# Adding the global keys of batch 0 by short matmuls instead of copying their value rows

**The chip, the cores and the metric.** One core of one Trainium2 chip (trn2). The metric is the device time of one execution in microseconds (us), from the core's first to its last instruction plus a constant start and end; lower is better. Most executions of one kernel lie within 0.3% of each other, so each one is measured against runs of the kernel before on the same chip. "Faster" and "slower" below mean only that the 95% interval of the ratio leaves 1 out.

Engines: PE is TensorE (matmuls), PEld its weight loads, DVE VectorE, ACT ScalarE, POOL GpSimd, SP SyncE. `L670` is line 670 of the kernel at hand; the same statement has another line number before and after.

## The reference, cut to what matters

```python
batch, n_heads, seq, head_dim = (8, 8, 576, 64)      # q, k, v
n_global = 8                                         # global_idx: 8 sorted positions
mask = np.abs(pos[:, None] - pos[None, :]) <= 32     # a window of 32 to each side ...
mask = mask | is_global[:, None] | is_global[None, :]  # ... plus 8 global rows and columns
attn = softmax(where(mask, q @ k.T / sqrt(64), -1e9))
x = (attn @ v).transpose(0, 2, 1, 3).reshape(4608, 512)
h = x @ w_in                                         # 512 -> 2048
out = (maximum(h, 0) ** 2) @ w_out                   # 2048 -> 512
```

So every query sees its window and the eight global keys. The kernel lays the keys of a batch out in five tiles of 128 rows. Rows 0 to 7 of each tile are the global keys, the others are window keys. One matmul with 128 contraction rows then adds both kinds.

## The kernel before

Attention runs batch by batch, in four pairs of heads, each in two halves of the queries. Everything from batch 1 on fills PE with expert units (`x @ w_in` and `g @ w_out`, in pieces held in a queue). Batch 0 has little expert work to put beside it, so its own chain is exposed there. That chain begins with the global value rows, which are not known by position until the index has been read (the code is cut, and comments are added):

```python
    def pick_values():                       # one-hot matmuls: the 8 global rows of V
        gp = pst("mm", [P, 512])[0:NG]
        for x in range(NT):
            nc.tensor.matmul(gp.rearrange(...), oh[:, x, :], vb[0][:, x, 0 : 2 * H : 2],
                             start=(x == 0), stop=(x == NT - 1))
        dve.tensor_copy(out=gv16, in_=gp.rearrange("p (h d) -> p h d", d=D))

    def spread_values(b, op, tiles=range(NT)):     # ... into rows 0..7 of the value tiles
        for x in tiles:
            op(out=vb[b][0:NG, x, 0 : 2 * H : 2], in_=gv16)
# ... (cut)
    pick_values()
    spread_values(0, dve.tensor_copy, range(0, 4))
    spread_values(0, act.copy, range(4, NT))
    masked(0, ets[2], WIN)
    masked(0, ets[3], WIN)
    # ... (cut: load issues on POOL, then:)
    next_in_place()                          # POOL casts gathered rows for batch 2
    keep_warm(SCHED["w7"])                   # fillers on PE
    half0_out(0, "mm")                       # outputs and reciprocals, pairs 0 to 3
    half0_out(1, "sc")
    half0_out(2, "acc")
    half0_out(3, "mm")
    # ... (cut: scores of half 1 of pairs 0, 1)
    scatter(0, 0)                            # global query columns into xT, half 0
    # ... (cut: half 1 of the four pairs, expert units between them)
    scatter(0, 1)
    take(len(queue) - SCHED["keep"])         # all queued expert units but `keep`
```

The sums of the softmax come from the same matmuls with a tile of ones in place of V; ACT takes a logarithm and an exponential of minus it to get the reciprocal. `scatter` copies eight columns per half into `xT`, the input of the expert units, so no expert unit of that half can start before it.

The softmax here doesn't subtract the row's maximum and nothing guards it: scores larger than these inputs give would overflow.

## Time and profile before

| | kernel before |
|---|---|
| time, median of the runs first given | 326.37 us |
| PE busy, share of the span | 97% |
| granted clock | 1.00 |
| picks start (L449) | 15.91 us |
| first expert unit starts | 25.79 us |
| first scatter | 23.86 to 25.74 us |
| second scatter | 36.08 to 38.53 us |

The table of waits gives, for each group, who it waited for, then the us in total, how often, and the longest. These are its lines for PE that the change could touch:

```profile
PE mm L543 <- DVE xT L751: 1.8, 2, 1.2
...
PE mm L524 <- DVE xT L751: 0.5, 1, 0.5
...
PE mm L670 <- DVE vb L457: 0.4, 1, 0.4
```

The two waits of L543 are those for the two scatters of batch 0, L524's is for the scatter of batch 1, and L670's is for the copied rows. Together 2.7 us.

### The profile page before, as it was taken

How to read it: one execution, taken by the hardware profiler on the slowest of the kernel's cores; microseconds unless marked ns; L12 is line 12 of the kernel's file. 1: busy time of each engine (PE TensorE's matmuls, PEld its weight loads, DVE VectorE, ACT ScalarE, POOL GpSimd, SP SyncE). 2: the span in 40 equal slices, each digit the busy share in tenths (PEclk: the TensorE clock that was granted, in tenths of full speed). 3: DMA queues.
4: the chain of work that ended last, by engine and by line, in shares of the span. 5: the costliest groups of instructions: out<-in, count | busy, mean ns of one | idle time of the engine just before them, and what ended most of it. 6: DMA issues, size and time to landing. Idle time of an engine off the chain costs nothing.

```text
span 326.0 us, 6920 instructions
## 1 busy us (share of the span) xinstructions
PE 316.8 (97%) x2434; PEld 164.5 (50%) x2434; DVE 227.0 (70%) x674; ACT 214.4 (66%) x418; POOL 110.2 (34%) x148
## 2 busy tenths in 40 slices
PE   6998999999999999999999999999999999999996
PEld 2645775445555455455545544454455544444444
DVE  7786987677878875987598758885888675313421
ACT  6677985569954995499549954995499636404600
POOL 9824663639800870089107700680000000000000
PEclk9999999999999999999999999999999999999999
DMA  8999999999994999399959996999610011011012
GB/s 186 176 204 190 174 186 167 154 147 107 153 131 141 73 138 171 134 83 139 132 162 82 148 126 144 98 134 132 139 60 0 34 58 39 2 73 56 2 54 75
DMA packets 148229, 37.53 MB, mean 115 GB/s; under 512 B 136171, under 2 KB 143715, under 8 KB 148195
## 3 DMA queue, kind: packets, MB, share of 16 engines
q0 software_dynamic: 105168, 17.93, 78.9%
q1 hardware_dynamic: 42880, 19.04, 30.3%
q8 instruction: 19, 0.31, 0.4%
q10 hardware_dynamic: 146, 0.13, 0.1%
q14 instruction: 16, 0.12, 0.1%
HBM read 37.30 MB, written 17.05 MB: 167 GB/s over the span
## 4 chain that ended last, share of the span: by engine, by line
PE 88%; DVE 7%; ACT 2%; issue 1%; DMA 1%
PE mm L587 29%; PE mm L524 26%; PE tr L524 9%; PE tr L587 7%; PE sc L679 3%; PE acc L679 3%; PE sc L627 3%; PE mm L543 2%; PE acc L627 2%; DVE xT L751 2%; PE tr L197 1%; DVE vb L457 1%; PE sc L670 1%; DVE xT L732 1%; ACT rec L702 1%
## 5 line engine op out<-in xcount | busy, mean ns | idle before, releaser
L587 PE MATMUL mm<-w_out,gt 128*128 128x512 f16 x448 | 104.4, 379 | 0.0
L524 PE MATMUL mm<-xT,w_in 128*128 128x512 f16 x384 | 90.8, 379 | 0.5 <-DVE xT L751 0.5
L587 PEld LDWEIGHTS <-gt 128*128 128x128 f16 x560 | 52.4, 98 | 58.6
L524 PEld LDWEIGHTS <-w_in 128*128 128x128 f16 x512 | 47.5, 98 | 53.7 <-issue 0.8
L529 ACT ACTIVATE rl<-mm 128x512 f16<-128x512 f32 x96 | 54.3, 599 | 26.7 <-PE mm L524 26.7
L530 DVE TENSOR_TENSOR gt<-rl 128x512 f16<-128x512 f16 x128 | 51.0, 422 | 17.0 <-ACT rl L529 15.6
L636 ACT ACTIVATE et<-sc 128x880 f16<-128x880 f32 (+1 forms) x32 | 29.0, 907 | 44.1 <-PE sc L627 39.1
L643 DVE TENSOR_TENSOR et<-et,mask 128x880 f16<-128x880 f16 (+1 forms) x64 | 38.9, 615 | 24.1 <-ACT et L636 23.8
L113 POOL DMA_DIRECT2D vb<-in_v_dram x40 | 40.7, 1532 | 9.0 <-DMA w_in<-in_moe_w_in_dram 7.3
L524 PE MATMUL tr<-xT,w_in 128*128 128x512 f16 x128 | 33.0, 380 | 0.0
L564 DVE COPY ot<-mm 128x512 f32<-128x512 f32 (+1 forms) x29 | 19.7, 680 | 18.0 <-PE mm L587 16.3
L636 ACT ACTIVATE et<-acc 128x880 f16<-128x880 f32 (+1 forms) x32 | 29.1, 909 | 1.0 <-PE acc L627 1.0
L703 ACT ACTIVATE rec<-rec 128x288 f32<-128x288 f32 x64 | 28.3, 443 | 2.0
L732 DVE TENSOR_TENSOR xT<-sc,rec 64x288 f16<-64x288 f32 (+1 forms) x55 | 25.0, 455 | 6.5 <-ACT rec L703 6.2
L732 DVE TENSOR_TENSOR xT<-acc,rec 64x288 f16<-64x288 f32 (+1 forms) x55 | 25.0, 455 | 3.9 <-ACT rec L703 1.1
L404 POOL DMA_DIRECT2D scr_k<-in_k_dram x30 | 26.6, 1111 | 2.8 <-issue 2.8
L679 PEld LDWEIGHTS <-vb 128*128 128x128 f16 x288 | 21.3, 98 | 11.5
L930 POOL COPY pin<-gsh 1x1 f32<-1x1 f32 x5 | 0.9, 177 | 76.4 <-DVE gsh L720 76.4
L702 ACT ACTIVATE rec<-sc 64x288 f32<-64x288 f32 (+1 forms) x55 | 22.3, 406 | 6.2 <-PE sc L679 4.2
L404 POOL DMA_DIRECT2D scr_q<-in_q_dram x24 | 25.1, 1585 | 3.0 <-DMA w_out<-in_moe_w_out_dram 3.0
L587 PE MATMUL tr<-w_out,gt 128*128 128x512 f16 x112 | 25.3, 379 | 0.0
L702 ACT ACTIVATE rec<-acc 64x288 f32<-64x288 f32 (+1 forms) x55 | 22.2, 404 | 2.0 <-PE acc L670 1.1
(147 smaller groups left out, 308.5 us busy)
## 6 DMA issues: line engine op xcount, KB each, us to landing
out_dram<-ot SPq DMA_DIRECT2D x35, 256.0 KB
vb<-in_v_dram POOLq DMA_DIRECT2D x32, 120.0 KB, 11.3
scr_q<-in_q_dram POOLq DMA_DIRECT2D x24, 144.0 KB, 5.9
scr_k<-in_k_dram POOLq DMA_DIRECT2D x24, 120.0 KB, 4.2
w_in<-in_moe_w_in_dram POOLq DMA_DIRECT2D x4, 512.0 KB, 11.9
w_out<-in_moe_w_out_dram POOLq DMA_DIRECT2D x4, 512.0 KB, 12.3
natk<-in_k_dram POOLq DMA_DIRECT2D x3, 288.0 KB, 10.9
natq<-in_q_dram POOLq DMA_DIRECT2D x3, 288.0 KB, 15.8
```

The lines of the kernel that those rows point to most:

```text
L113: pool.dma_start(out=vb[b][NG : NG + KN[x], x, 2 * hs.start : 2 * hs.stop : 2], in_=v[b, hs, x * KT : x * KT + KN[x]].rearrange("h s d -> ...
L404: pool.dma_start(out=scr[(nm, b % 2)][x * pitch + off : x * pitch + off + hi - lo].rearrange("s (h d) -> s h d", d=D), in_=src[nm][b, :, l ...
L524: nc.tensor.matmul(ph, w_in[:, t, u * P : (u + 1) * P], xT[:, t, XOFF + c * TC : XOFF + (c + 1) * TC], start=(t == 0), stop=(t == NDM - 1),)
L529: nc.scalar.activation(out=rl, in_=ph, func=AF.Relu)
L530: nc.vector.tensor_tensor(out=gts[c][:, u, :], in0=rl, in1=rl, op=ALU.mult)
L587: nc.tensor.matmul(po, gts[c][:, f, m * P : (m + 1) * P], w_out[:, f, :], start=(f == 0), stop=(f == NFF - 1),)
L636: act.activation(out=et[:, :, 0:W], in_=sc[:, :, 0:W], func=AF.Exp, bias=0.0, scale=scale)
L643: dve.tensor_tensor(out=et[:, :, 0:W], in0=et[:, :, 0:W], in1=mask[:, MB[half] : MB[half] + W].unsqueeze(1).to_broadcast((P, 2, W)), op=AL ...
L679: nc.tensor.matmul(banks[e][:, o : o + w], vtf[:, t, vo : vo + P], et[:, e, so : so + w], start=(n == 0), stop=(n == nw - 1), skip_group_c ...
L702: act.activation(out=rec[r], in_=av[xs][rs, :, 0:GTOK], func=AF.Ln)
L703: act.activation(out=rec, in_=rec, func=AF.Exp, scale=-1.0)
L732: dve.tensor_tensor(out=xT[r, hp, x0 : x0 + HS].rearrange("p (k x) -> p k x", k=2), in0=av[x][r, :, 0:GTOK], in1=rec[r], op=ALU.mult,)
```

## The change

Its intent: take the copies out of the chain. The value tiles keep zeros in rows 0 to 7. The eight rows stay in `gv16`, and matmuls with a contraction of 8 (K=8) add the global keys to each output afterwards. The window part of the outputs need not wait for them, nor need the denominators. With the time gained, fillers are taken out.

```diff
-SCHED = dict(... w7=4, wa=4, wb=3, wc=3, ... w=5, h0=0, ... h2=1, h3=0, keep=1, ...)
+SCHED = dict(... w7=0, wa=4, wb=2, wc=1, ... w=3, h0=1, ... h2=0, h3=0, keep=2, ...)
-    def pick_values():
-        gp = pst("mm", [P, 512])[0:NG]
+    def pick_values(part):                   # two picks of four heads each
+        gp = pst("mm", [P, 512])[0:NG, 0:256].rearrange("p (h d) -> p h d", d=D)
... (cut)
+    def global_keys(i, half, et, banks, wins):
... (cut: own = the column ranges of the three windows whose global keys are in use)
+        for n, (off, lo_, hi_) in enumerate(own):
+            for e in range(2):
+                nc.tensor.matmul(
+                    banks[0][D * e : D * e + D, lo_ - half * BANKC : hi_ - half * BANKC],
+                    gv16[:, 2 * hp + e], et[0:NG, e, off + lo_ : off + hi_],
+                    start=False, stop=(n == len(own) - 1), skip_group_check=True,
+                )
... (cut)
-    pick_values()
-    spread_values(0, dve.tensor_copy, range(0, 4))
-    spread_values(0, act.copy, range(4, NT))
     masked(0, ets[2], WIN)
-    masked(0, ets[3], WIN)
+    pick_values(0)
+    pick_values(1)
+    first = [pst("mm", [P, 512]), pst("tr", [P, 512])]
+    column_outputs(0, 0, ets[0], first, WIN, slice(None))
... (cut: load issues, next_in_place() as before)
-    keep_warm(SCHED["w7"])
-    half0_out(0, "mm")
... (cut)
+    reciprocals(0, first, True)
+    second = output_banks("sc")
+    column_outputs(1, 0, ets[1], second, WIN, slice(None))
+    masked(0, ets[3], WIN)
+    global_keys(0, 0, ets[0], first, WIN)
+    global_keys(1, 0, ets[1], second, WIN)
... (cut: pairs 2 and 3 with their global_keys; half 1 likewise)
```

More of the change, by code (lines that the diff above doesn't have):

```diff
@@ L42 @@
 MB = (0, 456)
-SCHED = dict(w8=2, w9=3, w5=3, w6=0, w7=4, wa=4, wb=3, wc=3, g0=1, w0=2, w1=4, w2=2, w3=2, w4=3, w=5, h0=0, h1=1, h4=1, h5=1, h2=1, h3=0, keep=1, b1=((3, 1, 3), (2, 1, 3), (2, 1, 3), (2, 1, 2)), last=((2, 1, 4), (3, 1, 4), (2, 1, 4), (2, 1, 7)))
+SCHED = dict(w8=2, w9=3, w5=3, w6=0, w7=0, wa=4, wb=2, wc=1, g0=1, w0=2, w1=4, w2=2, w3=2, w4=3, w=3, h0=1, h1=1, h4=1, h5=1, h2=0, h3=0, keep=2, b1=((3, 1, 3), (2, 1, 3), (2, 1, 3), (2, 1, 2)), last=((2, 1, 4), (3, 1, 4), (2, 1, 4), (2, 1, 7)))
 ONES = 2.0**-7 * (1.0 + 15360.0 / 2**23)
@@ L444, in clear_value_rows @@
         )
-    def pick_values():
-        gp = pst("mm", [P, 512])[0:NG]
+    def pick_values(part):
+        gp = pst("mm", [P, 512])[0:NG, 0:256].rearrange("p (h d) -> p h d", d=D)
+        hs = slice(4 * part, 4 * part + 4)
         for x in range(NT):
             nc.tensor.matmul(
-                gp.rearrange("p (h d) -> p h d", d=D), oh[:, x, :], vb[0][:, x, 0 : 2 * H : 2],
+                gp, oh[:, x, :], vb[0][:, x, 8 * part : 8 * part + 8 : 2],
                 start=(x == 0), stop=(x == NT - 1),
             )
-        dve.tensor_copy(out=gv16, in_=gp.rearrange("p (h d) -> p h d", d=D))
+        dve.tensor_copy(out=gv16[:, hs], in_=gp)
     def spread_values(b, op, tiles=range(NT)):
@@ L654, with output_banks, column_outputs @@
     PARTS = (((lo, 0, hi, 0), (hi, 1, lo, 1)), ((slice(0, P), 0, slice(0, P), 1),))
-    def outputs(i, half, et, tag, wins, columns=False):
-        b, hp = divmod(i, NHP)
-        if tag == "mm":
-            banks = [pst("mm", [P, 512]) for _ in range(2)]
-        else:
-            acc = pst(tag, [P, 2, 512])
-            banks = [acc[:, x] for x in range(2)]
-        vt = vb[b]
-        vtf = vt.rearrange("p t x d -> p t (x d)")
+    def output_banks(tag):
+        if tag == "mm":
+            return [pst("mm", [P, 512]) for _ in range(2)]
+        acc = pst(tag, [P, 2, 512])
+        return [acc[:, x] for x in range(2)]
+    def column_outputs(i, half, et, banks, wins, some):
+        b, hp = divmod(i, NHP)
         nw = len(wins[half])
-        for n, (t, so, c0, w) in enumerate(wins[half] if columns else ()):
+        for n, (t, so, c0, w) in list(enumerate(wins[half]))[some]:
             o = c0 - half * BANKC
@@ L671, in outputs @@
                         banks[x][D * e : D * e + D, o : o + w],
-                        one64 if x else vt[:, t, 4 * hp + 2 * e], et[:, e, so : so + w],
-                        start=(n == 0), stop=(n == nw - 1), skip_group_check=True,
-                    )
-        for e in () if columns else range(2):
+                        one64 if x else vb[b][:, t, 4 * hp + 2 * e], et[:, e, so : so + w],
+                        start=(n == 0), stop=(n == nw - 1 and (b > 0 or x > 0)),
+                        skip_group_check=True,
+                    )
+    def global_keys(i, half, et, banks, wins):
+        b, hp = divmod(i, NHP)
+        own = []
+        for t, so, c0, w in wins[half]:
+            cs = [
+                (max(KT * t + 8 * grp, GRP * grp, c0),
+                 min(KT * (t + 1) + 8 * grp, GRP * grp + GTOK, c0 + w))
+                for grp in range(4)
+            ]
+            cs = [c for c in cs if c[0] < c[1]]
+            if cs:
+                own.append((so - c0, cs[0][0], cs[-1][1]))
+        for n, (off, lo_, hi_) in enumerate(own):
[5 more added lines that the diff above has]
+                )
+    def outputs(i, half, et, tag, wins, columns=False):
+        b, hp = divmod(i, NHP)
+        banks = output_banks(tag)
+        if columns:
+            column_outputs(i, half, et, banks, wins, slice(None))
+            if b == 0:
+                global_keys(i, half, et, banks, wins)
+            return banks
+        vt = vb[b]
+        vtf = vt.rearrange("p t x d -> p t (x d)")
+        nw = len(wins[half])
+        for e in range(2):
             for n, (t, so, c0, w) in enumerate(wins[half]):
@@ L694, in global_outputs, with reciprocals @@
             )
+    recs = {}
+    def reciprocals(i, acc, columns):
+        rec = recs[i] = sbt("rec", [P, 2, GTOK], FP32, bufs=4)
+        for r, x, rs, xs in PARTS[columns]:
+            den = acc[xs][rs, 0:BANKC].rearrange("p (k c) -> p k c", c=GRP)
+            act.activation(out=rec[r], in_=den[:, :, 0:GTOK], func=AF.Ln)
+        act.activation(out=rec, in_=rec, func=AF.Exp, scale=-1.0)
     def finish_outputs(i, half, acc, columns=False):
@@ L699, in finish_outputs @@
         av = [a[:, 0:BANKC].rearrange("p (k c) -> p k c", c=GRP) for a in acc]
-        rec = sbt("rec", [P, 2, GTOK], FP32, bufs=4)
-        for r, x, rs, xs in parts:
-            act.activation(out=rec[r], in_=av[xs][rs, :, 0:GTOK], func=AF.Ln)
-        act.activation(out=rec, in_=rec, func=AF.Exp, scale=-1.0)
+        if i not in recs:
+            reciprocals(i, acc, columns)
+        rec = recs.pop(i)
         if b == 0:
@@ L712, in finish_outputs @@
                     )
-                if hp >= NHP - 2:
-                    a, z = (0, NHP - 1) if hp < NHP - 1 else (NHP - 1, NHP)
-                    global_outputs(0, gsum[0], a, z, columns)
+                if hp == NHP - 1:
+                    global_outputs(0, gsum[0], 0, NHP, columns)
         else:
@@ L784, in half0 @@
         ets[i] = exps(0, scores(i, 0, tag, WIN), WIN)
-    def half0_out(i, tag):
-        acc = outputs(i, 0, ets[i], tag, WIN, columns=True)
-        finish_outputs(i, 0, acc, columns=True)
     half0(0)
@@ L822 @@
     next_in_place()
-    keep_warm(SCHED["w7"])
-    half0_out(0, "mm")
-    half0_out(1, "sc")
-    half0_out(2, "acc")
-    half0_out(3, "mm")
+    reciprocals(0, first, True)
[4 more added lines that the diff above has]
+    global_keys(1, 0, ets[1], second, WIN)
+    finish_outputs(0, 0, first, columns=True)
+    finish_outputs(1, 0, second, columns=True)
+    for i, tag in ((2, "acc"), (3, "mm")):
+        finish_outputs(i, 0, outputs(i, 0, ets[i], tag, WIN, columns=True), columns=True)
     def half1(i):
```

## The prediction

> **What bounds the kernel now.** I read the page first, then the chain of waits in order of time for the stretch 14 to 50 us, then the timeline around it, the table of waits, and the busy table by stretch. First lines of the page and two lines of the busy table (us, then each engine's busy time):
>
> ```profile
> PE 316.8 (97%) x2434; PEld 164.5 (50%) x2434; DVE 227.0 (70%) x674; ACT 214.4 (66%) x418; POOL 110.2 (34%) x148
> ...
> 15.00:20.00 5.00, 4.03 (x69) 2.21 (x63) 3.20 (x12) 3.19 (x6) 2.45 (x4) 1.00 1.27 205
> 20.00:26.00 6.00, 4.84 (x72) 2.59 (x67) 5.36 (x26) 5.64 (x13) 1.82 (x2) 1.00 1.28 204
> ```
>
> TensorE (PE) is busy for 97% of the span. From 46 us to the end nothing but PE work counts; the change touches none of that. Only a stretch in which PE is idle, or busy with nothing of use, can give time back, and batch 0 is one: between 15 and 26 us PE is idle 2.1 us, and part of its busy time is filler (L197, matmuls on an idle tile that only keep the clock up). The chain there (start, us, what):
>
> ```profile
> 15.97 1.19 PE mm L449 x5
> 17.16 0.02 issue
> 17.18 0.69 DVE gv L453
> 17.88 0.02 issue
> 17.90 1.33 DVE vb L457 x4
> 19.23 0.04 issue
> 19.27 0.32 PE mm L670 x8
> 19.59 0.02 issue
> 19.62 0.42 ACT rec L702
> ...
> 25.79 1.03 PE mm L543 x8
> ```
>
> The eight global value rows are picked (L449), copied to fp16 (L453), copied into rows 0 to 7 of five value tiles (L457), and only then can the outputs of pair 0 (L670) end and their reciprocals (L702, L703) start. After that ScalarE (ACT) and VectorE (DVE) pass four pairs, DVE scatters the global columns (L751), and at 25.79 the first expert unit (L543) starts. The timeline shows what DVE could have done meanwhile, and who waited for the scatter:
>
> ```profile
> 17.18 0.68 DVE L453 CAST gv<-mm 8x512 f16<-8x512 f32 x1 [1.76 <-PE mm L449]
> ...
> 19.14 1.15 DVE L643 TENSOR_TENSOR et<-et,mask 128x912 f16<-128x912 f16 x2
> ...
> 25.79 1.03 PE L543 MATMUL mm<-xT,w_in 128*128 128x256 f16 x8 [1.16 <-DVE xT L751]
> ```
>
> DVE idles 1.76 us ahead of the copy although one of the two masks (L643, et of pair 2) could be had from 16.4 on: its exponential starts at 15.41 and takes 0.95.
>
> **What the Trainium skill says.** "TensorE: Matmul & The Clock Gate", section "Why this matters for your kernels": a matmul with 32 contraction rows takes as long as one with 128. So I price the K=8 matmuls by their columns. The trace has no K=8 matmul, but it gives the price of columns: in the pair of column outputs from 19.42 on, two matmuls of 160 columns for both heads start 0.07 us after the ones before, 192 columns 0.08, 88 and 8 columns 0.03 to 0.035.
> The same page, Part 1: an idle window of about 3.4 us halves the clock. The trace shows a granted clock of 1.00 through an idle gap of 1.16 us. Nine fillers go, but no gap gets near 3.4 us, so I expect the clock to stay 1.00.
> "PSUM — Partial Sum Buffer", section "PSUM bank collisions raise a hardware error": two engines must not touch one bank at once. The trace agrees: DVE's sum of pair 1 (L709) starts at 20.91, after ACT's logarithm of the same bank (20.41, 0.39). So ACT paces the four pairs, at 0.77 us each (20.41, 21.18, 21.95).
> "SBUF — State Buffer", section "Who interferes with whom": DVE copies that use the shared port pair and GpSimd (POOL) shut each other out. The trace agrees: the eight copies of the second scatter (36.08) take 2.45 us beside three POOL casts, and one of the first takes 0.42 instead of 0.19 beside a POOL issue at 24.23. Without it the first scatter is 8 x 0.21 = 1.7 us.
>
> **The change part by part.**
> (1) Removed: the five row copies, 1.33 us of DVE on the chain and 0.62 of ACT beside it.
> (2) The pick becomes two picks of half the columns: ten matmuls, the same 1.1 to 1.2 us of PE. The copy becomes two of 256 columns. 8x512 takes 0.68; taking 0.15 of that as fixed, a half is 0.42, so 0.8 for both: 0.1 more.
> (3) Moved: the mask of pair 2 goes ahead of the copies, into the 1.76 us idle (0.6 saved). The outputs of pair 0 go directly behind the picks on PE, with denominators in another bank than values, and its reciprocal no longer waits for any global row.
> (4) Added: six K=8 matmuls per pair and half, 120, 128 and 48 columns in half 0, 72, 128 and 96 in half 1: about 0.05 + 0.055 + 0.033 = 0.14 us for both heads; eight times, 1.1 us of PE.
> (5) The two small global divisions (L690, L692) become one: 0.20 + 0.17 less, 0.05 more for its extra columns.
> (6) Fillers on PE: w7 4 to 0, wb 3 to 2, wc 3 to 1, w 5 to 3: nine fewer at 0.21 = 1.9 us. One expert unit moves between the two half-1 outputs (h0) from behind pair 2 (h2), and one more stays queued for batch 1 (keep 2), which hands the same PE work on.
>
> New path, step by step: picks end near 17.1; DVE masks pair 2 at 16.4 to 17.0, copies to about 17.75, masks pair 3 to 18.3. PE passes pair 0's outputs by 17.5 and pair 1's by 18.0, then the global matmuls of both by 18.3. ACT takes the logarithm of pair 0 at 17.7 instead of 19.62. Pair 1's logarithm must wait for its global matmuls, as its banks are one tile: 18.5. Then ACT's pace: 18.5, 19.27, 20.05 for pairs 1, 2 and 3, where the kernel before has 20.41, 21.18 and 21.95: 1.9 us earlier. The last exponential ends at 20.9; sum, division, last product: 21.8; scatter 1.7: 23.5. The first expert unit starts at 23.5 instead of 25.79: 2.3 us earlier.
>
> From there to the scatter of half 1 it is PE that counts. Two fillers fewer (0.4) against four times 0.13 of global matmuls: 0.1 to 0.2 later. So the half-1 outputs end some 2.1 us earlier, near 32.5. One unit that ran before batch 1's scores now runs behind them; as PE is full from there on, that is neutral, if it fills the wait for the second scatter. Before, PE idled 0.64 us for that scatter; here I allow 0.3 for the scores of the first pair of batch 1, which must wait for a bank, and nothing else.
>
> The sum in PE time between 15 and 46 us, as a second count: fillers -1.9, global matmuls +1.1, idle from about 2.8 (0.97 + 1.16 + 0.64) to about 1.7. That is -1.9 us. The two counts agree on **1.9 us, so 324.5 us**.
>
> **The rivals.**
> R1, the loads become the bound. GpSimd's issues wait for the transfer eight places back, which gives landing times: w_in's four parts at 18.20, 20.40, 24.23 and 26.60, the first values of batch 1 at 34.72. The expert units that use w_in would run at 23.5 at the earliest on parts 1 and 2, and near 30 on part 3: landed. The batch-1 values are nearer: from 34.72 to 45.85, where the third w_out part lands, four value parts and three of w_out went through; at 2.1 us per w_out part (as w_in) the values take 1.2 each, so the last lands near 39.4. Its first use would move from 42.6 to about 40.1. It just fits; if it doesn't, 0.5 to 1 us is lost: 325.3.
> R2, the global matmuls cost more than their columns (a weight load of few rows that does not hide, 12 instructions in a burst). At 0.3 us instead of 0.14 eight times this takes 1.3 back, some of it in gaps: 325.4.
> R3, the second scatter keeps its end. It sits beside POOL casts whose start hangs on loads (35.5 to 37.2), not on compute; moved 2 us ahead it may meet a w_out issue as well as the casts, and PE, out of units of half 0, waits: 0.3 to 0.7 lost. For: the 2.45 us above. Against: with keep 2 there is one unit more to fill.
> R4, everything hidden by PE: the page's 97% speaks for it, but the 2.1 us idle and the fillers lie in this very stretch, so I give it little: 326.2.
> R5, better than thought: the gap for the scatters vanishes altogether: 323.8.
>
> **Range and chances.** Centre 324.5; R1 to R3 pull up by up to 1 us, R5 down by 0.7; eight in ten: **323.6 to 325.6**. Two per cent is 6.5 us, more than all idle and filler of the stretch together, so faster by over 2% gets 0.01, slower 0.01 (only if a wait or cold clock appeared that I don't see), within 2% gets 0.98.
>
> **What would show it.** The chain without vb L457; ACT's first logarithm near 17.7 and the next near 18.5; L751 ending near 23.5 and the first L543-type unit there; six K=8 matmuls in 0.14 us; fewer idle us of PE between 15 and 40 (about 1.7 in all); half-1 scatter ending 2 us or more earlier; clock 1.00. Wrong would be: a first unit after 24.3, PE waiting for DMA of vb between 38 and 41, more than 0.25 us per burst of global matmuls, or a shift of 2 us at 34 us that is gone at 50.

## More of the kernel before

The chain of waits in half 1 (start, us, what) shows what outputs without global matmuls take there:

```profile
26.82 0.50 PE sc L670 x12
27.33 0.75 PE tr L197 x3
28.08 0.50 PE acc L670 x12
```

Twelve output matmuls take 0.50 us, and three fillers (L197) stand between two pairs.

## The result, and the profile after

The changed kernel took **326.98 us** (median of 4 runs, 326.90 to 327.12) against 326.60 us of the kernel before (4 runs, 326.36 to 327.01): ratio 1.0011, 95% interval 0.9994 to 1.0028. It is correct, and the verdict is "same" (within 2%). A ratio here is always the mean time of one kernel's fast runs over that of the other's of the same rounds, so it is not quite the ratio of the medians beside it.

The change stayed within 2%, as forecast, but the 1.9 us did not come out, and 326.98 lies outside the range of 323.6 to 325.6. The page and the busy table by stretch (start:end, length, then busy us and count of PE, PEld, DVE, ACT, POOL, then granted clock, DMA share, GB/s):

```profile
PE 317.3 (98%) x2478; PEld 166.1 (51%) x2478; DVE 226.1 (70%) x669; ACT 214.3 (66%) x417; POOL 110.2 (34%) x148
...
15.00:20.00 5.00, 4.30 (x112) 3.57 (x112) 3.19 (x12) 3.33 (x8) 2.48 (x4) 1.00 1.26 202
20.00:26.00 6.00, 5.41 (x58) 2.86 (x59) 4.52 (x19) 5.34 (x11) 1.82 (x2) 1.00 1.28 204
```

PE has more busy time than before, 317.3 against 316.8 us, although nine fillers are gone. That already suggests that the work put in costs more than the 1.1 us counted for it. The chain of waits:

```profile
14.89 1.18 PE mm L450 x10
16.07 0.19 PE mm L670 x2
16.26 0.07 PE tr L670
16.33 0.69 issue
17.02 0.26 PE tr L670
...
17.66 0.42 ACT rec L735
...
23.67 1.03 PE mm L544 x8
24.70 0.50 PE sc L670 x12
25.20 0.25 PE sc L691 x6
```

The row copies are gone from the chain, as intended, and pair 0's outputs start at 16.07, directly behind the picks. But after three matmuls PE stands still for 0.69 us, and the chain can name no releaser for it ("issue"). In half 1 each pair now has a line of L691, the global matmuls: 0.25 us for six, where 0.14 was counted. The waits of PE that answer to those of before:

```profile
PE mm L544 <- DVE xT L791: 1.2, 2, 0.6
PE tr L670 <- issue: 0.7, 1, 0.7
...
PE sc L670 <- DVE vb L458: 0.4, 1, 0.4
PE sc L712 <- DVE et L644: 0.2, 1, 0.2
```

They sum to 2.5 us, and with a 0.2 us wait for L772 to the same 2.7 us as before: the waits have changed their names, not their sum. And the timeline at the second scatter, DVE beside POOL:

```profile
34.53 2.75 DVE L791 COPY xT<-gx 128x4 f16 x8
...
34.89 0.60 POOL L370 CAST g16sk<-grows 8x512 f16<-8x512 f32 x1
...
37.34 1.05 PE L544 MATMUL mm<-xT,w_in 128*128 128x256 f16 x8 [0.57 <-DVE xT L791]
```

The two profiles cannot be laid over each other by time of day: in the profiled execution of the kernel before the index arrived 0.9 us later than in the others, and all behind it with it. So I count from the start of the picks in each trace (us, read from the traces):

| from the start of the picks | before | before, 2nd profile | after | after, 2nd profile |
|---|---|---|---|---|
| first logarithm | 3.71 | 3.28 | 2.84 | 2.83 |
| logarithm of pair 3 | 6.05 | 5.62 | 5.38 | 5.37 |
| first expert unit | 9.88 | 9.60 | 8.85 | 8.84 |
| second scatter starts | 20.17 | 19.89 | 19.71 | 19.70 |
| second scatter ends | 22.62 | 22.54 | 22.47 | 22.52 |
| end | 310.14 | 310.48 | 310.45 | 310.67 |

The first unit is 0.75 to 1.0 us earlier, not 2.3; of this 0.2 to 0.45 is left when the second scatter starts, 0.1 when it ends, and nothing at the end. There are thus three places to explain: the way to the first logarithm, the stretch between the scatters, and the second scatter with what follows.

### The profile page after: what moved, and what is told of

It is laid out like the page before. It is cut to its first block, busy times and chain, and to the rows that moved or that the text cites. A ratio compares the mean times of both kernels' runs of the same rounds, so it can differ in the third digit from the quotient of the medians.

```text
span 325.3 us, 7001 instructions
## 1 busy us (share of the span) xinstructions
PE 317.3 (98%) x2478; PEld 166.1 (51%) x2478; DVE 226.1 (70%) x669; ACT 214.3 (66%) x417; POOL 110.2 (34%) x148
## 4 chain that ended last, share of the span: by engine, by line
PE 91%; DVE 5%; ACT 2%; issue 1%
PE mm L588 29%; PE mm L525 26%; PE tr L525 9%; PE tr L588 7%; PE mm L544 4%; PE sc L712 3%; PE acc L712 3%; PE sc L628 3%; PE acc L628 2%; DVE xT L791 2%; PE tr L197 2%; ACT rec L736 1%; PE sc L670 1%; ACT rec L735 1%; DVE xT L772 1%
## 5 line engine op out<-in xcount | busy, mean ns | idle before, releaser
L531 DVE TENSOR_TENSOR gt<-rl 128x512 f16<-128x512 f16 x128 | 51.2, 422 | 17.1 <-ACT rl L530 15.6
L565 DVE COPY ot<-mm 128x512 f32<-128x512 f32 (+1 forms) x29 | 19.7, 680 | 17.7 <-PE mm L588 16.0
L772 DVE TENSOR_TENSOR xT<-sc,rec 64x288 f16<-64x288 f32 (+1 forms) x55 | 25.0, 455 | 7.3 <-ACT rec L736 6.9
L772 DVE TENSOR_TENSOR xT<-acc,rec 64x288 f16<-64x288 f32 (+1 forms) x55 | 25.0, 455 | 4.2 <-ACT rec L736 1.4
L712 PEld LDWEIGHTS <-vb 128*128 128x128 f16 x288 | 21.3, 98 | 12.3 <-issue 0.9
L404 POOL DMA_DIRECT2D scr_q<-in_q_dram x24 | 24.8, 1571 | 3.8 <-DMA w_out<-in_moe_w_out_dram 3.8
```

The costliest lines, as they stand in the source:

```text
L404: pool.dma_start(out=scr[(nm, b % 2)][x * pitch + off : x * pitch + off + hi - lo].rearrange("s (h d) -> s h d", d=D), in_=src[nm][b, :, l ...
L531: nc.vector.tensor_tensor(out=gts[c][:, u, :], in0=rl, in1=rl, op=ALU.mult)
L712: nc.tensor.matmul(banks[e][:, o : o + w], vtf[:, t, vo : vo + P], et[:, e, so : so + w], start=(n == 0), stop=(n == nw - 1), skip_group_c ...
L772: dve.tensor_tensor(out=xT[r, hp, x0 : x0 + HS].rearrange("p (k x) -> p k x", k=2), in0=av[x][r, :, 0:GTOK], in1=rec[r], op=ALU.mult,)
```

## The experiments

Five series ran, on chips 8, 6, 3, 10 and 10. The first four have their own runs of the kernel before (medians 327.33, 326.59, 326.55 and 327.17 us). The fifth uses the eleven of the fourth and one more (327.21), so its ratios are not all from the same rounds. All kernels gave correct results.

### First series: repeats, the standstill, and half 1

**b_again** and **a_again**: the two kernels unchanged, for a second profile each.

> The kernel before, unchanged, for a second profile. In its first profile the index load landed late: VectorE's first use of it (L217) ran at 2.86 us, in the profile of the changed kernel at 1.97, and everything up to the picks is 1.08 us later (picks at 15.97 against 14.89). Theory: this is luck of one load, so a second profile has L217 near 2.0, the picks near 14.9 and a span near 324.6. Rival: the new code makes the head faster; then the picks are near 16.0 again.

> The changed kernel, unchanged. Theory: counted from the picks on it loses 0.4 us (310.4 against 310.0), so the time is 0.1% to 0.2% above before; TensorE stalls again for 0.7 to 0.9 us between the first and the second matmul on the second bank of pair 0, with no semaphore waited for, and each burst of global matmuls in half 1 costs 0.24 us. Rival: the stall is luck of one execution; then it is gone here and the time is 0.7 us lower than in the first runs.

Measured: 327.17 us (one run) and 328.12 us (6 runs, 327.39 to 329.07), ratio of a_again 1.0027 (1.0011 to 1.0043). The changed kernel is a little slower on this chip. Its standstill is there again, 0.68 us at the same matmul; the kernel before has none in its second profile either.

**a_fill**: three fillers between the picks and pair 0's outputs. If PE stands still because its next instructions have not arrived, fillers there cost nothing; if it is short of time, they cost 0.65 us.

```diff
+    keep_warm(3)
     first = [pst("mm", [P, 512]), pst("tr", [P, 512])]
```

> The changed kernel with three filler matmuls (0.65 us) between the picks and the outputs of pair 0. Theory F (TensorE runs out of fetched instructions there: a 16 KB instruction transfer[...] starts at 14.69, 0.2 us before the picks, and TensorE goes on 2.3 us later): the fillers run while the next instructions are still on their way, so they cost at most 0.3 us of the 0.65: the first logarithm 2.8 to 3.1 us after the picks' start (2.77 in the changed kernel), the total the same within 0.3 us; the stall is shorter and lies 6 instructions earlier in the program. Rival B (something holds the second bank until about 17.0): the first logarithm also stays, but the stall stays between the same two matmuls on that bank. Rival C (the stall is a fixed pause that comes with these matmuls): the first logarithm comes 0.65 us later and the stall stays 0.7.

Measured: 327.78 us (4 runs, 327.69 to 327.86), ratio 1.0011 (0.9997 to 1.0026). Its chain of waits:

```profile
14.91 1.18 PE mm L450 x10
16.09 0.77 PE tr L197 x3
16.86 0.11 issue
16.97 0.26 PE mm L670 x2
...
17.69 0.42 ACT rec L735
```

The fillers take the place of the standstill, and the first logarithm comes 2.85 us after the picks' start, as in the changed kernel (2.84). So those 0.65 us were of no use to the outputs. What PE may be waiting for can be read from the transfers: on the queue of kind instruction there are 19 transfers of 16,384 bytes in the whole run, and one of them starts at the picks. In all sixteen traces of the changed kernel and its variants this transfer starts between 0.33 us before and 0.05 us after the picks, and PE goes on 2.2 to 2.5 us after that start, whether the standstill is 0.48 or 0.97 us long. Counted over all instructions recorded for PE, the same number, 450, start before PE goes on in each of the sixteen, a_fill included, where the next one is another matmul because of the three fillers. That speaks against rival B (the stall would have stayed between the same two matmuls) and rival C (the first logarithm would have come 0.65 us later). In the kernel before the same transfer starts 0.35 us ahead of the picks, and the row copies and fillers lie over it. I take this as an instruction fetch of PE. That the transfer and the restart move together, and that the place is the same by count, is shown; the profile itself names no cause.

**a_rows**: no global matmuls in half 1; the rows are copied into three value tiles by ACT, off the chain, and ACT's casts of the global k and q rows are put later.

```diff
-            if b == 0:
+            if b == 0 and half == 0:
                 global_keys(i, half, et, banks, wins)
...
     half1(0)
+    spread_values(0, act.copy, range(2, 3))
     keep_warm(SCHED["wa"])
     half1(1)
+    spread_values(0, act.copy, range(3, NT))
     scatter(0, 0)
-    globals_in_place("k")
-    globals_in_place("q")
...
     half1_out(0)
+    globals_in_place("k")
...
     half1_out(1)
+    globals_in_place("q")
```

> The changed kernel, with the global keys as K=8 matmuls in half 0 alone. For half 1 ScalarE copies the rows into value tiles 2 to 4 (three copies of 0.6 us) between its exponentials of half 1, where it waits anyway, and the casts of the batch-1 globals move behind. Theory K (the bursts of half 1 cost 0.24 us each on a busy TensorE): four bursts less, so the scatter of half 1 and the end come 0.7 to 1.0 us earlier, 326.0 us. Rival A (ScalarE, not TensorE, sets the pace of half 1): the copies and the moved casts delay the reciprocals and less than 0.4 us is gained, or none.

Measured: 328.53 us (6 runs, 327.78 to 330.81), ratio 1.0047 (1.0023 to 1.0071): slower. The second scatter starts only 0.15 us earlier (19.55 against 19.70), and PE now waits twice 0.49 us for masks. The experiment moved ACT work into that chain as well, so it doesn't price the bursts. It only says that copies on ACT are no way out.

### Second series: the casts, the unit order, the contraction

**a_casts** and **b_casts**: POOL's three casts for batch 2 behind the second scatter instead of beside it, in the kernel after and in the kernel before.

```diff
-    next_in_place()
...
+            next_in_place()
             tokens_to_scratch(2)
```

> The changed kernel; GpSimd's three casts of the batch-1 globals (0.6 us each), which lie beside the second scatter, are put behind it. Theory S (the second scatter of eight copies takes 2.75 us instead of 1.7 because GpSimd and VectorE shut each other out, and TensorE has no units left and waits for it): the scatter takes 1.7 to 2.0 us, TensorE's wait of 0.57 us for it goes, and the kernel gets 0.6 to 1.0 us faster. Rival: the scatter shortens but TensorE then waits for something else (row copies of batch 1, loads), and less than 0.3 us is gained.

> The same edit of the kernel before. Theory S: its second scatter goes from 2.45 (2.65 in the second profile) to 1.7 to 2.0 us, TensorE's wait of 0.64 (0.85) shrinks, 0.4 to 0.9 us faster. If this and the edited changed kernel gain the same, the casts are not what the change ran into but a cost of both.

Measured: 327.07 us (6 runs), ratio 1.0013 (0.9999 to 1.0028), and 326.65 us (6 runs), ratio 1.0006 (0.9986 to 1.0026): nothing gained. The second scatter falls to 1.85 and 1.82 us and PE no longer waits for it, as the theory says. But the casts then stand beside the next DVE copies. The timeline and the waits of a_casts:

```profile
37.07 0.81 POOL L370 CAST g16sk<-grows 8x512 f16<-8x512 f32 x1
...
38.28 1.88 DVE L458 COPY vb<-gv 8x512 f16<-8x512 f16 x3
...
PE sc L670 <- DVE vb L458: 1.2, 2, 0.9
```

The row copies of batch 1 take 1.88 us (1.32 in the changed kernel), and PE waits 1.2 us for them. The wait has moved, which was the rival.

**a_units**: the old place of the expert unit and the old number held back.

```diff
-SCHED = dict(... h0=1, ... h2=0, h3=0, keep=2, ...)
+SCHED = dict(... h0=0, ... h2=1, h3=0, keep=1, ...)
```

> The changed kernel with the expert units of half 1 where the kernel before has them (h0 0, h2 1, keep 1). From the end of the first scatter to the start of the second the changed kernel takes 10.9 us, the kernel before 10.3. Theory U (the unit put ahead of pair 2's outputs stands on the chain to the second scatter, where in the kernel before it ran beside ScalarE's reciprocals): the stretch shrinks to 10.1 to 10.7 us, the second scatter comes 0.2 to 0.8 us earlier; with one unit less to fill the wait TensorE idles there, so the time moves by -0.5 to +0.3 us. Rival (the bursts of global matmuls alone make it longer): the stretch stays 10.9 or grows.

Measured: 326.80 us (7 runs, 326.58 to 328.99), ratio 1.0005 (0.9991 to 1.0019). Its second scatter starts 13.14 us after the end of the first, but the profiled execution was the slowest of the seven (328.99 us, mean clock 0.989), and can't be read for that. The busy table of a_units shows why (clock third from the end):

```profile
18.00:20.00 2.00, 2.00 (x63) 1.85 (x59) 1.14 (x6) 1.92 (x5) 0.92 (x1) 0.88 1.27 208
20.00:22.00 2.00, 2.00 (x28) 1.04 (x26) 1.66 (x9) 1.34 (x4) 0.92 (x1) 0.50 1.25 205
```

The granted clock fell to a half from 19.5 to 26.4 us, and the first unit came at 11.18. In the 10 us before the fall the longest idle gap of PE was 0.97 us, so it is not the idle window of 3.4 us that the prediction took from the Trainium skill; its cause stays open. It fell in this one of all the profiles; two untraced runs, of a_rows (330.81 us) and of k128_early (327.01), have a mean clock of 0.995 and are the slowest of their kernels. All three have fewer fillers than the kernel before, whose own runs show no mean clock under 0.998, but three of some ninety runs don't show that the fillers are the reason. Either way it is a matter of single executions and not the cause of the result.

**a_k128**: the global matmuls with 128 contraction rows instead of 8. `gv16` gets zeros in rows 8 to 127, so the result is the same; the columns, the number of matmuls and the chain are untouched.

```diff
-    gv16 = sbt("gv16", [NG, H, D], FP16)
+    gv16 = sbt("gv16", [P, H, D], FP16)      # pool.memset(gv16, 0.0) early
-                    gv16[:, 2 * hp + e], et[0:NG, e, off + lo_ : off + hi_],
+                    gv16[:, 2 * hp + e], et[:, e, off + lo_ : off + hi_],
```

> The changed kernel with the global matmuls over all 128 rows: the value rows padded with zeros, the same columns. A burst between its neighbours now costs 0.24 us in half 1, while its six matmuls start within 0.12 to 0.14. Theory R (the extra is the switch of the array from 128 rows to 8 and back): the burst costs 0.13 to 0.16 us and pairs 2 and 3 of half 0 take 0.1 us less each; the time falls by at most 0.3 us, as TensorE then waits for others. Rival (the extra belongs to any group of other weights, or to the wait for the accumulation): 0.24 us again.

Measured: 326.60 us (4 runs, 325.99 to 326.95), ratio 1.0001 (0.9984 to 1.0019). In its chain of waits:

```profile
24.89 0.13 PE sc L691 x6
...
26.72 0.13 PE acc L691 x6
```

A burst takes 0.13 us instead of 0.25. Counted in the traces from the first output matmul to the next other instruction, the four pairs of half 1 take 0.505, 0.505, 0.406 and 0.505 us without global matmuls (before), 0.751, 0.751, 0.749 and 0.728 with K=8, and 0.636, 0.636, 0.537 and 0.635 with 128 rows. In half 0 all outputs take 2.40 us before (second profile), 3.45 with K=8 and 2.96 with 128 rows, the standstill subtracted. So the eight bursts cost 1.06 + 1.06 = **2.1 us with K=8, and 0.52 + 0.57 = 1.1 us with 128 rows**. The half-1 figures repeat within 0.03 us in every trace. Those of half 0 are rougher, since waits for the row copies lie in the 2.40 us, and in a_fill, where no standstill cuts the outputs, they take 3.20 us with K=8 instead of 3.45. The difference between the two contractions, 0.5 us in each half, doesn't rest on that. The 1.1 us of the prediction is about what full contraction costs; the short contraction doubles it. The starts show where the time goes: in half 1 of the changed kernel the first K=8 matmul starts 0.15 us after the last output matmul pair (24.98 to 25.13); with 128 rows it is 0.06 (24.67 to 24.73). The six themselves start within 0.12 us with K=8, and within 0.09 with 128 rows.

Yet one microsecond less of PE work did not show in the time: the standstill is 0.96 us here, the wait for the first scatter 0.92, and that for the second scatter, which takes 2.91 us beside the casts, 0.73.

### Third series: the casts earlier

The casts are free to go elsewhere, as POOL waits between its load issues.

**k128_early**: a_k128 with the three casts spread over those waits, from 27 to 32 us. **b_early**: the same in the kernel before.

```diff
     for x in range(NT):
         fetch_values(1, x)
+        if x == 3:
+            next_in_place("k")
     for j in range(4):
         pool.dma_start(out=w_out[:, ts(j, 4), :], in_=wo[:, ts(j, 4), :])
-    next_in_place()
+        if j < 2:
+            next_in_place("qv"[j])
```

> Global keys with 128 contraction rows (zeros below the eight global rows), and the three GpSimd casts of the gathered rows spread over GpSimd's waits between its load issues (start 26.5 to 32 us) instead of beside the second scatter. Theory that the second scatter's end is held by those casts: the scatter takes 1.8 to 1.9 us instead of 2.9, PE's wait for it (0.73 in a_k128) is gone, the masks of batch 1 behind it keep 1.14 and no new wait of 0.5 us appears, as nothing is shifted onto them: 0.5 to 0.9 us less than a_k128, ratio to before 0.997 to 0.999. Rival (something else holds batch 1, e.g. its value loads or the pace of ScalarE behind it): the wait moves to another line and the ratio stays 0.9995 to 1.0015.

> The kernel before with the same spreading of the casts alone. If the casts cost time in this stretch whatever the change: scatter 1.8 instead of 2.45 to 2.65, wait of 0.45 to 0.64 us gone, 0.3 to 0.6 us less, ratio 0.998 to 0.999. If the rival holds: 0.9995 to 1.001.

Measured: k128_early 325.08 us (6 runs, 324.87 to 327.01), **ratio 0.9962 (0.9940 to 0.9984)**, the first kernel that is faster than the kernel before beyond its interval. b_early 327.00 us (6 runs, 325.58 to 327.70), ratio 1.0013 (0.9996 to 1.0031): no gain. The timeline of k128_early:

```profile
30.09 0.60 POOL L370 CAST g16sq<-grows 8x512 f16<-8x512 f32 x1
...
33.95 1.82 DVE L791 COPY xT<-gx 128x4 f16 x8
...
36.01 1.14 DVE L644 TENSOR_TENSOR et<-et,mask 128x880 f16<-128x880 f16 x2
37.06 0.80 DVE L458 COPY vb<-gv 8x512 f16<-8x512 f16 x3
```

The scatter takes 1.82 us, and the masks (1.14) and row copies (0.80) behind it keep their time as well. PE waits for one scatter only (0.9 us, the first), and the second ends 20.94 us after the picks, 1.6 us earlier than before. b_early's profiled execution, at 325.58 us its fastest, shows the same: its second scatter takes 1.94 us, and the wait for it is gone. But its other five runs are 0.8 to 2.1 us slower. They were not traced, so why it doesn't keep the gain stays open.

**k128_units** and **k128_early_units**: a_k128 and k128_early with the unit order of a_units.

> a_k128 with the expert unit put back behind pair 2 (h0 0, h2 1) and one unit held back instead of two. Theory that the unit ahead of pair 2's outputs costs about 1 us of the stretch between the scatters: second scatter starts 0.5 to 1 us earlier after the first one's end than in a_k128 (10.6 us), but PE waits for it longer by the same, as one unit less... is held: time within 0.3 us of a_k128. A half clock for some us in one execution, as in a_units, is possible; then first unit 2 us later.

> Both. If casts and unit order are independent: the scatter takes 1.85 us and starts 0.5 to 1 us earlier than in k128_early, the wait behind it is under 0.3; the best of the four: ratio 0.996 to 0.998. If not (batch 1 held by loads or ScalarE): no better than k128_early, within 0.2 us.

Measured: 326.30 us (6 runs), ratio 0.9986 (0.9972 to 1.0000), and 325.80 us (6 runs), ratio 0.9984 (0.9963 to 1.0005). From the first scatter's end to the second's start k128_units takes 10.43 us and a_k128 10.56; the other two take 10.43 and 10.57. The place of the unit is therefore worth 0.1 us, and the 1 us that I expected from the chains is refuted.

### Fourth series: the square of four on one chip

Until here the parts had been compared across chips. The four combinations of contraction and casts in the changed kernel, on one chip in the same rounds: **a_third** (neither), **k128_again** (128 rows), **a_early** (early casts), **k128_early2** (both). The edits are those above.

> The changed kernel once more, as the first corner of a square of four: ratio to before 1.001 to 1.003 as in its two earlier measurements.

> 128 contraction rows alone. If the gain was held back by the casts behind the second scatter (theory): the bursts save about 1.2 us of PE, but PE then waits 0.7 to 0.9 us for the scatter: 0.3 to 0.5 us less than a_third. If 128 rows are the whole cure and a_k128 had bad luck: 1.2 us less.

> Spread casts alone, with K=8. If the two count only together: second scatter 1.85 us, but the bursts keep PE busy till later, so its wait of 0.57 us alone goes: 0.3 to 0.6 us less than a_third. If the casts are the whole cure: as fast as k128_early2, 1.2 to 1.5 us less.

> Both, a repeat of k128_early on another chip: ratio to before 0.995 to 0.998. If that result was luck of its chip: 0.999 to 1.001.

| against before (327.17 us) | casts beside the scatter | casts early |
|---|---|---|
| K=8 | 327.85 us, 1.0017 (1.0000 to 1.0034) | 326.89 us, 0.9996 (0.9972 to 1.0020) |
| 128 rows | 327.38 us, 1.0010 (0.9992 to 1.0027) | 326.79 us, 0.9974 (0.9953 to 0.9995) |

In ratios times 327.2 us: 128 rows alone give 0.2 us, early casts alone 0.7, both 1.4. Both together are the repeat of k128_early, again faster than before beyond the interval. That the two are worth 0.5 us more together than singly fits the traces: k128_again waits 0.68 us for the second scatter, which is most of what its bursts save. But 0.5 us is inside the intervals, so it isn't settled. Nor does a profile show where the early casts' 0.7 us come from: in a_third's the second scatter took only 2.06 us beside the casts, and PE did not wait for it.

All four profiles hold a wait that none of the earlier ones has at this length, here from the waits of k128_early2:

```profile
PE sc L712 <- DVE et L644: 1.7, 1, 1.7
```

These are the first outputs of batch 2, 53 us behind the picks. The exponential ahead of the mask starts 2.2 to 2.4 us after its scores in these four, 0.24 us after them in the profiles of before, after and k128_early. The profile shows ACT idle and no wait that would explain it (in a_third its idle time of 3.23 us is put down to something remote). The kernel before has the late exponential as well (1.66 us in b_again), but there PE has something else to do or to wait for. In the profiles it goes by chip: the exponential starts 0.8 to 2.4 us after its scores in all ten on chips 8 and 10 (first, fourth and fifth series), with either kernel and either `keep`, and 0.24 us after them in all ten of the other series and of the first result.

### Fifth series: is it `keep` that exposes PE?

**k128_early_keep1**: one unit held back for batch 1 instead of two; **k128_early3**: the best version a third time.

```diff
-SCHED = dict(... keep=2, ...)
+SCHED = dict(... keep=1, ...)
```

> The best version with one expert unit held back instead of two. If keep 2 exposes PE to the late exponential of batch 2: its single runs spread by less than 1 us, the wait of 1.5 to 1.7 us ahead of the first outputs of batch 2 does not occur, ratio 0.995 to 0.997. If not, or if the one unit less leaves PE waiting for the second scatter: same as k128_early3 or 0.3 us slower.

> The best version a third time: ratio 0.996 to 0.998, single runs spread over up to 2 us where the late exponential comes and goes.

Measured: k128_early_keep1 **326.11 us (6 runs, 325.73 to 326.37), ratio 0.9963 (0.9947 to 0.9979)**; k128_early3 326.63 us (6 runs, 325.44 to 326.77), ratio 0.9971 (0.9952 to 0.9990). In the profiled execution of keep1 the exponential was late by 1.66 us, as in b_again, and no wait of L712 followed. PE had two short waits instead, of which one is in the waits as

```profile
PE mm L525 <- DVE xT L791: 0.5, 1, 0.5
```

that is, the wait for the scatter of batch 1 that the kernel before has too. In k128_early3 the exponential was 2.2 us late and PE waited 1.5 us for it. Its single runs lie at 325.44 once and at 326.44 to 326.77 five times, those of keep1 within 0.64 us. So in the traces PE waits for a late exponential with two units held back (0.8 us or more in all seven profiles where it was over 1 us late) and not with one (b_again and this run); the difference of the two ratios is inside their intervals. Why the exponential is late on two chips and not on the others stays open.

k128_early, measured three times, and k128_early_keep1, measured once, are the versions that are faster than the kernel before. The latter wins 1.1 us by the medians of its chip; which of the two is better isn't settled.

## Why the prediction was wrong

Two terms of its sum failed: the price of the global matmuls, 2.1 us instead of 1.1, and the idle time of PE, which was to fall by 1.1 us and did not fall. By its own steps:

- **"ACT takes the logarithm of pair 0 at 17.7 instead of 19.62": wrong.** That is 1.8 us after the picks' start; it came at 2.84. Of the 1.0 us missing, 0.7 is the standstill of PE behind the picks, which a_fill shows to be no lack of PE time. The prediction had removed the fillers and copies that lay over it without asking what else lay under them. No part of the sum had this term. The other 0.3 lies in the outputs of pair 0 on PE: 0.7 us in a_fill, where the prediction allowed 0.4 (17.1 to 17.5). Counted on from the kernel before, the first unit then stands at 15.91 + 8.85 = 24.8, past the 24.3 that the prediction had named as a sign of being wrong.
- **"Then ACT's pace": nearly right.** Predicted 2.35 us from the first logarithm to that of pair 3, measured 2.54 with K=8, and 2.37 in a_k128 (3.10 to 5.47). With K=8 the bursts pace it too, not ACT alone.
- **"Scatter 1.7": right**, 1.66 us (2.0 to 2.1 in a_third and k128_early2).
- **"Global matmuls +1.1": the term that was mis-sized; R2 was the right rival.** Eight bursts measured 2.1 us with K=8. With 128 contraction rows they measure 1.1. So the price by columns was right, and the step "I price the K=8 matmuls by their columns" failed for K=8 between matmuls of 128 rows.
- **"Two fillers fewer against four times 0.13: 0.1 to 0.2 later": wrong.** From the first scatter's end to the second's start it took 10.91 us instead of 10.34, 0.57 later; 10.56 with 128 rows. Three bursts of that stretch cost 0.25 + 0.25 + 0.34 = 0.84 us; with the 0.1 us of the moved unit, less the two fillers, that makes up the 0.57.
- **"Half-1 scatter ending 2 us or more earlier": wrong; R3 held.** The casts kept the scatter at 2.75 us, and it ended 0.1 us earlier. The prediction named this collision and gave it 0.3 to 0.7 us. What it missed is that a scatter starting earlier only moves into more of the casts: it began 0.57 us after the first of them before (36.08 and 35.51), and 0.36 us ahead of it after (34.53 and 34.89).
- **"That hands the same PE work on": right for the place of the unit, wrong for `keep`.** The place moved the second scatter by 0.1 us only (k128_units). But keep 2 lets the late exponential of batch 2 reach PE, 1.5 to 1.7 us in five of the profiles. That fits the ratios of the changed kernel, 1.0027 and 1.0017, on the two chips where a late exponential reached PE in a profile of it or of a variant with keep 2 (0.8 to 1.7 us), but single runs without a profile don't show it.
- **R1 (loads): did not happen.** No wait of PE for a DMA of `vb` stands in any profile's table of waits.
- **The clock: right in the mean, not always.** 1.00 in the profile after; a half for 6.8 us in one execution of a_units.

The second count of the prediction, in PE time, goes: fillers −1.9 as predicted, bursts +2.1 instead of +1.1, idle 2.7 to 2.7 instead of 2.8 to 1.7. The sum is +0.2 us instead of −1.9, and the measured difference of the medians is +0.4. The two counts of the prediction agreed since both rested on the same unmeasured price and on the same picture of free waits.

Of the four places of the Trainium skill in the prediction: the one on small contractions failed as I used it (last section), the clock held but for the one execution, and the PSUM bank order and the port shared by DVE and POOL held, the latter with the 1.82 us of k128_early's scatter against 2.91 in a_k128.

## What to carry to other kernels

A short contraction was not free here, between full ones: if the operand can be padded with zeros at no cost, give all matmuls of a stream the same contraction. Before taking time out of a chain, list what runs beside the part removed (instruction transfers, casts on a port that is shared, late work of another engine), for each of these can be the next wait. And move such side work to an engine's own idle time ahead of the critical copy: behind it, it met the next copy here.

## What the Trainium skill lacked or had wrong

- "TensorE: Matmul & The Clock Gate", section "Why this matters for your kernels": that a single matmul of 32 contraction rows takes as long as one of 128 doesn't carry over to a burst between full ones. Six K=8 matmuls cost 0.25 us in half 1, the same six with 128 rows 0.13, eight bursts 2.1 against 1.1 us. No page gives the cost of changing the contraction in a stream; "TensorEngine Tiling (Array Packing)", section "Key Properties", says without a figure that changing the tiling mode drains TensorE, and no run here shows whether these bursts change it.
- "Runtime: NRT & Kernel Launch", section "Instruction fetch mechanics", says that an engine fetches its instructions in blocks of 16 KiB and that the cost of crossing a block is mostly hidden. If the standstill is such a crossing, as I take it, it was not hidden here: PE stands still for 0.48 to 0.97 us behind the picks without any semaphore, and goes on 2.2 to 2.5 us after the start of a transfer of 16,384 bytes on the instruction queue. No page tells how to see this in a profile.
- No page has it: the exponential of batch 2 that starts 0.24 us after its scores in ten profiles and 0.8 to 2.4 us after them in the ten on chips 8 and 10, with no wait in the profile that explains it.
